# Chunk 1's second layer as seven half-size products, with batch 2's scaling of v spread over the first layer

## Chip, cores and metric

The kernel runs on one core of one Trainium2 chip. The metric is the device time of one launch in microseconds (us). Before the change it is 316.57 us, the median of 3 runs (316.44 to 317.22).

The core has five engines, each working through its own list of instructions in order: PE (TensorE: matmuls and transposes), DVE (VectorE), ACT (ScalarE), POOL (GpSimd) and SP (here only a queue that issues DMA transfers). They wait for each other by semaphores. PE writes its results into PSUM, which has eight banks; a bank can be written again only when its readers are done.

## What is computed

Attention with a decay, over 8 batches of 8 heads, 576 positions, 64 dimensions, and behind it a two-layer network with an exact GELU over all 4608 tokens:

```python
scores = scale * np.matmul(q, k.transpose(0, 1, 3, 2))
cum = np.cumsum(np.maximum(s, 0.0), axis=-1)
bias = -(cum[:, :, :, None] - cum[:, :, None, :])
scores = np.where(causal, -1000000000.0, scores + np.minimum(bias, 0.0))
attn = softmax(scores)
attn_out = np.matmul(attn, v)

x = attn_out.transpose(0, 2, 1, 3).reshape(4608, 512)
h = x @ w_in
g = 0.5 * h * (1.0 + erf(h / sqrt(2.0)))
out = g @ w_out
```

`w_in` is 512 x 2048, `w_out` 2048 x 512.

## The kernel before

**Chunks and batches.** The network runs over nine chunks of 512 tokens (`c` = 0 to 8), the attention over eight batches of 576 tokens. The loop over `c` (L748) computes chunk `c`'s two layers, and in between the attention of batch `nb = c + 1`, whose result (`xT`, a ring of 1536 token columns) the next chunks read. The order of all instructions is written out by hand; nothing is scheduled by a planner, so each engine's list is the program's order.

**First layer.** `l1_item(c, f2)` (L535) does eight matmuls of 128 x 128 by 512 columns into one of three pairs of banks X, Y, Z, and ACT applies GELU into `gT` (L551; the last item in two halves, L554). There are eight items, `f2` = 0 to 7. `order[c]` says which pair each third item takes; the same pairs hold scores and attention results in the second layer.

**Second layer, plain.** `l2_item(c, sub, f0, f1)` (L556) adds up 16 matmuls of 512 columns for each of four blocks of 128 tokens, 64 matmuls in all, into one of the single banks `M[0]`, `M[1]`; DVE or ACT copies the bank to `o_sb` and SP stores it. Chunks 0 and 1 use it.

**Second layer by seven products.** Chunks 2 to 8 split the 512 x 2048 by 2048 x 512 product into halves each way and use seven half-size products in place of eight, a Strassen-Winograd scheme. `prod(c, i, ...)` (L610) is one product: 16 matmuls of 256 columns, 112 in all. `sums_a` (L599) makes the sums of halves of `gT` on DVE (tiles `Ss`), four formulas over two halves of the inner dimension; `sums_b` (L591) made those of `w_out` (tiles `Ts`) during chunk 0. The first halves need the GELUs of items 0 to 3, the second halves those of items 4 to 7. The products share two banks: `al` (`M[0]`) is copied to `kept` three times along the way, and three additions on DVE put the output together. The `kept` tiles share buffers with the loads of q and k that batches 0 to 2 use.

**Attention of batch `nb` inside the second layer.** `sc_mm` (L421): scores of two heads into a pair of banks, exponential on ACT (L435); `mask` (L439) on DVE; `av_pe`, `av_out`, `av_tails` (L483 to L525): the product with v, logarithm and exponential on ACT, multiplication into `xT` on DVE (L498). v is first multiplied by weights of the decay: `scale_v` (L242) on DVE, reading `raw_v`, writing `vv`. `squares_v` (L233) adds up the squares of v on ACT and `absmax` (L227) the largest entries of q and k on DVE, for a certificate at the end.

**How q and k come in.** Batches 0 to 2 are transposed by PE (`tr_two`, `tr_one`, L401 to L417), batch 2 in the first layer of chunk 1: after each of the items 2 to 5, 36 transposes into the two banks `M` and two DVE copies (L399) out of them into `qkT`. Batches 3 to 7 go another way: POOL loads raw q and k (L197), casts them (`cast_qk`, L201), and at the start of the chunk before their use SP issues five DMA transposes into `qkT[nb % 2]` (`transpose_tiles`, L212). A small POOL operation behind the transposes (`behind_g`, L146, L763) holds back POOL's loads of the batch after, and a small SP transfer behind those (`behind`, L142, L792) holds back SP's loads of v (`load_v`, L220).

**Chunk 1 before.** It has a branch of its own (L892 to L919): plain second layer; all five tiles of batch 2's v are scaled after item 5 of the first layer (L778), then `squares_v(2)` and `load_v(3)`; the reductions `absmax(1, 2)` and `absmax(1, 3)` stand after the third block's matmuls (L914, L915), between the two halves of the attention.

Of the kernel before, what the change touches and what calls it, by code (L numbers as in the profile page):

```python
# [19 lines left out]
def kernel(  # L20
# [173 lines left out]
    def load_qk(b, n):  # L194
        raws[b, n] = t = work.tile([128, ST, H, D], fp32, tag=f"raw{n}", bufs=1, name=f"raw_{n}")
        for st, n_st, src in tiles(q if n == "q" else k, b):
            nc.gpsimd.dma_start(out=t[:n_st, st], in_=src)  # L197
# [22 lines left out]
    def load_v(b, engs):  # L220
        raws[b, "v"] = t = work.tile(
            [128, ST, H, D], fp32, tag="rawk" if b == 1 else "rawv", bufs=1, name="raw_v"
        )
        for st, n_st, src in tiles(v, b):
            engs[st % len(engs)].dma_start(out=t[:n_st, st], in_=src)
# [169 lines left out]
    def copy(eng, out, in_):  # L395
        if eng is nc.scalar:
            eng.copy(out, in_)
        else:
            eng.tensor_copy(out, in_)  # L399
# [348 lines left out]
    for c in range(NCH):  # L748
        nb = c + 1
        if c < 2:  # L750
            l1_item(c, 0, 0, KO - 2)
            l1_item(c, 1, 0, KO - 2)
            av_tails(c, M[0])
            l1_item(c, 0, KO - 2)
            l1_item(c, 1, KO - 2)
        else:
            l1_item(c, 0, 0, KO - 2)
            l1_item(c, 0, KO - 2)
            l1_item(c, 1)
        if 1 < c and nb < B:  # L760
            transpose_tiles(nb)
            if nb + 1 < B:
                behind_g(qkT[nb % 2][0:1, 1, NP - 1, S - 1 : S])  # L763
                for n in "qk":
                    load_qk(nb + 1, n)
        for p in range(NP) if c in (0, B - 1) else (0, 1) if c == 1 else (0, 1, 2) if c < B else ():
            absmax(c, p)
        if c == B:
            cert_1()
        for f2 in range(2, FT // 2):  # L770
            l1_item(c, f2)
            if c == 1 and 2 <= f2 < 6:
                tr_two(2, f2 // 2 - 1, f2 % 2, both)
            if c == 1 and f2 == 2:
                squares_v(1)
                load_qk(3, "k")
            if c == 1 and f2 == 5:
                scale_v(2, STS, nc.vector)  # L778
                squares_v(2)
                load_v(3, [nc.sync])  # L780
            if c == B and f2 in (2, 4):
                (cert_2, cert_3)[f2 // 2 - 1](M[0])
            if c > 1 and f2 == 3:
                if nb < B:
                    scale_v(nb, [(0, 4), (4, 5)], nc.vector)
                sums_a(c, (1, 2, 3), 0, HF // 2)
                if nb < B:
                    absmax(c, 3)
            if c > 1 and nb < B and f2 == 4:
                squares_v(nb)  # L790
                if nb + 1 < B:
                    behind(2, raws[nb + 1, "k"][0:1, ST - 2, 0, :])  # L792
                    load_v(nb + 1, [nc.sync])
        if c == 0:
            squares_v(0)
            sums_b((1, 2, 3, 4), 0, 4)
            exp_set()
            x, y, z = order[0]
            l2_item(c, 0, 0, 8)
            l2_item(c, 1, 0, 8)  # L800
            tr_one(1, 0, 0, nc.vector, z)
            tr_one(1, 0, 1, nc.scalar, x)
            l2_item(c, 2, 0, 8, y)
            sc_mm(1, 0, (z, x))
            l2_item(c, 3, 0, 8, y)
            sc_mm(1, 1, (z, x))
            mask(1, 0, nc.vector)
            sums_b((1, 2, 3), 4, 8)
            behind(1, w_out_r[0:1, FT - 5, 0:D])
            load_v(1, [nc.sync])  # L810
            l2_item(c, 0, 8, 12)
            l2_item(c, 1, 8, 12)
            tr_one(1, 1, 0, nc.vector, z)
            tr_one(1, 1, 1, nc.scalar, x)
            mask(1, 1, nc.vector)
            sums_b((4,), 4, 8)
            behind_v(1, 1)
            for qd in range(2):
                for n in "qk":
                    load_front(2, n, qd)  # L820
            l2_item(c, 2, 8, 12)
            l2_item(c, 3, 8, 12)
            sc_mm(1, 2, (z, x))
            l2_item(c, 0, 12, eng=nc.scalar)
            sc_mm(1, 3, (z, x))
            mask(1, 2, nc.vector)
            scale_v(1, STS, nc.vector)
            l2_item(c, 1, 12, eng=nc.scalar)
            l2_item(c, 2, 12, eng=nc.scalar)
            mask(1, 3, nc.vector)  # L830
            av_main(1, 0, M[0], z)
            l2_item(c, 3, 12)
            av_main(1, 1, M[1], x)
            order[1] = (y, z, x)
            load_v(2, [nc.sync])
            load_qk(3, "q")
        elif c > 1 and nb < B:
            exp_set()
            sums_a(c, (1, 2), HF // 2, HF)

            x, y, z = order[c]
            order[nb] = (z, x, y)
            add = nc.vector.tensor_tensor
            al_t = bank(M[0], [128, 2, 256], fp32, "o_al")
            al = [al_t[:, u] for u in range(2)]
            kept = [keep_sb(i, n) for i, n in enumerate(("q0", "k0", "q1"))]
            oa = [two_sb() for _ in range(2)]

            prod(c, 1, al, start=True)
            sc_mm(nb, 0, (z, x))  # L850
            sc_mm(nb, 2, (y,))
            copy(nc.vector, kept[0], al_t)
            be = bank(M[1], [128, 2, 256], fp32, "o_be")
            prod(c, 2, [be[:, u] for u in range(2)], start=True)
            prod(c, 6, al, 0, 6)
            mask(nb, 0, nc.vector)
            add(oa[0][:, :, N1], be, kept[0], op=ALU.add)
            sc_mm(nb, 2, (z,), 1)
            sc_mm(nb, 1, (x, y))
            mask(nb, 2, nc.vector)  # L860
            prod(c, 6, al, 6)
            copy(nc.vector, kept[1], al_t)
            mask(nb, 1, nc.vector)
            sc_mm(nb, 3, (z, x))
            sums_a(c, (3, 4), HF // 2, HF)
            sums_a(c, (4,), 0, HF // 2)
            ga_t = bank(M[1], [128, 2, 256], fp32, "o_ga")
            ga = [ga_t[:, u] for u in range(2)]
            prod(c, 5, ga, start=True)
            mask(nb, 3, nc.vector)  # L870
            if nb + 1 < B:
                behind_g(P_of[nb, 3][0:1, 1, PW - 1 : PW])
                cast_qk(nb + 1)
            den = bank(z, [128, 2, 512], fp32, "av_d")
            o = av_pe(nb, 0, den[:, 0], y)
            av_out(nb, 0, den[:, 0], o)
            prod(c, 7, al)
            copy(nc.scalar, kept[2], al_t)
            o = av_pe(nb, 1, den[:, 1], x)
            add(oa[1][:, :, N2], ga_t, kept[2], op=ALU.add)  # L880
            av_out(nb, 1, den[:, 1], o)
            prod(c, 4, al)
            av_tails(nb, y)
            copy(nc.scalar, oa[1][:, :, N1], al_t)
            store(c, 2, oa[1])
            prod(c, 3, ga)
            add(oa[0][:, :, N2], ga_t, kept[1], op=ALU.add)
            store(c, 1, oa[0])
            square(c + 1 if c > 2 else 0)
            if c == 2:  # L890
                cert_decay()
        elif c == 1:  # L892
            exp_set()

            x, y, z = order[c]
            order[nb] = (y, z, x)
            l2_item(c, 0, 0, 8)
            sc_mm(nb, 0, (z, x))
            sc_mm(nb, 2, (y,))
            l2_item(c, 0, 8)  # L900
            mask(nb, 0, nc.vector)
            l2_item(c, 1, 0, 3)
            sc_mm(nb, 2, (z,), 1)
            sc_mm(nb, 1, (x, y))
            mask(nb, 2, nc.vector)
            l2_item(c, 1, 3, eng=nc.scalar)
            mask(nb, 1, nc.vector)
            sc_mm(nb, 3, (z, x))
            mask(nb, 3, nc.vector)
            behind_g(P_of[nb, 3][0:1, 1, PW - 1 : PW])  # L910
            cast_qk(3)
            av_main(nb, 0, M[0], y)
            l2_item(c, 2, slot=M[1])
            absmax(1, 2)  # L914
            absmax(1, 3)  # L915
            av_main(nb, 1, M[0], z)
            l2_item(c, 3, 0, 8)
            av_tails(nb, x)
            l2_item(c, 3, 8)  # L919
        else:  # L920
            if c == B - 1:
                order[c + 1] = order[c]
            sums_a(c, (1, 2), HF // 2, HF)
            l2_seven(c)
# [156 lines left out]
```

## Time and profile before

| what | us |
|---|---|
| median of 3 runs | 316.57 |
| the profiled execution | 316.66 |
| its span in the profile | 314.8 |
| PE busy | 296.7 (94%) |
| ACT busy | 237.2 (75%) |
| DVE busy | 205.1 (65%) |
| POOL busy | 98.7 (31%) |

The profile shows one execution. "L545" is line 545 of the kernel before. A row of the timeline is: start, duration, engine, line, operation, output<-input, shapes, count, and in brackets the idle time of the engine just before, with what ended it. In rows of the chain of waits the two numbers are the start and the time that this piece contributes to the chain. PEld is PE's loading of weights, which overlaps its matmuls. SPq and POOLq rows are issues of DMA transfers; they last as long as the issue takes, not the transfer. Ends of matmuls are modelled: of 16 narrow matmuls in a row the last one's pipeline is included, so the time per matmul is read from the chain or from start to start.

### The profile page before, as it was taken

How to read it: one execution, taken by the hardware profiler on the slowest of the kernel's cores; microseconds unless marked ns; L12 is line 12 of the kernel's file. 1: busy time of each engine (PE TensorE's matmuls, PEld its weight loads, DVE VectorE, ACT ScalarE, POOL GpSimd, SP SyncE). 2: the span in 40 equal slices, each digit the busy share in tenths (PEclk: the TensorE clock that was granted, in tenths of full speed). 3: DMA queues.
4: the chain of work that ended last, by engine and by line, in shares of the span. 5: the costliest groups of instructions: out<-in, count | busy, mean ns of one | idle time of the engine just before them, and what ended most of it. 6: DMA issues, size and time to landing. Idle time of an engine off the chain costs nothing.

```text
span 314.8 us, 8169 instructions
## 1 busy us (share of the span) xinstructions
PE 296.7 (94%) x3402; PEld 183.6 (58%) x3402; DVE 205.1 (65%) x405; ACT 237.2 (75%) x322; POOL 98.7 (31%) x180
## 2 busy tenths in 40 slices
PE   1789999999999999999999999999999999999991
PEld 1564444544554578547854785478547864874680
DVE  3786357775489487797885687668765874432560
ACT  3777787799955996989698978898779885656410
POOL 6574008023080646137621953095300000000000
PEclk9999999999999999999999999999999999999997
DMA  7999999987816596959698969776990030021013
GB/s 122 208 173 198 207 194 161 294 197 186 180 38 147 132 204 132 224 100 219 132 251 124 198 144 263 137 163 139 248 188 2 2 135 0 2 94 40 2 37 106
DMA packets 77964, 45.05 MB, mean 143 GB/s; under 512 B 63200, under 2 KB 70368, under 8 KB 77920
## 3 DMA queue, kind: packets, MB, share of 16 engines
q1 hardware_dynamic: 67136, 24.93, 34.4%
q0 software_dynamic: 10784, 19.53, 32.1%
q8 instruction: 28, 0.46, 0.6%
q14 instruction: 16, 0.13, 0.2%
HBM read 36.85 MB, written 9.44 MB: 147 GB/s over the span
## 4 chain that ended last, share of the span: by engine, by line
PE 85%; ACT 5%; DVE 4%; DMA 2%; issue 1%; POOL 0%; ACTq 0%; POOLq 0%
PE h_ps L545 39%; PE o_al L617 16%; PE o_ga L617 8%; PE o_ps L569 5%; PE sc_ps L429 5%; PE o_be L617 4%; PE av_o L458 4%; PE av_d L458 2%; DMA fk<-in_k_dram 2%; ACT junk L237 2%; ACT P L435 2%; DVE vv L247 2%; PE av_t L458 1%; PE tr_ps L390 1%; DVE qkT L399 1%
## 5 line engine op out<-in xcount | busy, mean ns | idle before, releaser
L545 PE MATMUL h_ps<-xT,w_in_r 128*128 128x512 bf16 x576 | 127.1, 379 | 0.5 <-DVE o_sb L399 0.5
L545 PEld LDWEIGHTS <-w_in_r 128*128 128x128 bf16 x576 | 55.7, 98 | 65.5 <-issue 0.8
L551 ACT ACTIVATE gT<-h_ps 128x1024 f16<-128x1024 f32 x63 | 62.7, 1020 | 24.7 <-PE h_ps L545 24.5
L435 ACT ACTIVATE P<-sc_ps 128x1024 bf16<-128x1024 f32 x64 | 60.3, 1030 | 3.2 <-PE sc_ps L429 3.2
L617 PEld LDWEIGHTS <-S 128*128 128x128 f16 x448 | 42.1, 98 | 6.7 <-issue 0.8
L229 DVE TENSOR_REDUCE amx<-qkT 128x2 f32<-128x1152 bf16 x32 | 41.5, 1344 | 0.1
L608 DVE TENSOR_TENSOR S<-gT 128x1024 f16<-128x1024 f16 x28 | 19.3, 688 | 31.3 <-ACT gT L554 24.0
L617 PEld LDWEIGHTS <-gT 128*128 128x128 f16 x336 | 32.0, 98 | 7.1 <-issue 1.8
L443 DVE TENSOR_TENSOR P<-P,tri_bf 128x512 bf16<-128x512 bf16 x64 | 25.9, 421 | 14.0 <-ACT P L435 13.5
L569 PE MATMUL o_ps<-w_out_r,gT 128*128 128x512 f16 x128 | 30.0, 380 | 0.0
L617 PE MATMUL o_al<-T,S 128*128 128x256 f16 x224 | 27.7, 273 | 0.0
L197 POOL DMA_DIRECT2D raw_k<-in_k_dram x25 | 21.1, 850 | 13.5 <-DMA raw_v<-in_v_dram 13.5
L429 PE MATMUL sc_ps<-qkT 64*128 64x256 bf16 (+2 forms) x320 | 22.2, 264 | 3.0 <-DVE qkT L399 1.7
L498 DVE TENSOR_TENSOR xT<-av_o,ln 128x256 bf16<-128x256 f32 (+2 forms) x72 | 23.6, 387 | 2.1 <-ACT ln L474 0.9
L247 DVE TENSOR_TENSOR vv<-raw_v,wb 128x512 bf16<-128x512 f32 (+2 forms) x25 | 23.7, 1001 | 0.0
L197 POOL DMA_DIRECT2D raw_q<-in_q_dram x25 | 21.1, 858 | 0.9 <-POOL seen_v L148 0.6
L429 PEld LDWEIGHTS <-qkT 64*128 64x128 bf16 x320 | 13.8, 99 | 12.6 <-issue 7.0
L237 ACT ACTIVATE junk<-raw_v 128x2048 bf16<-128x2048 f32 (+1 forms) x16 | 20.3, 1269 | 0.3
L569 PEld LDWEIGHTS <-gT 128*128 128x128 f16 x128 | 11.5, 98 | 13.6 <-issue 0.7
L399 DVE COPY qkT<-tr_ps 128x576 bf16<-128x576 bf16 (+1 forms) x15 | 12.0, 834 | 9.4 <-PE tr_ps L390 9.4
L474 ACT ACTIVATE ln<-ln,lnb 128x256 f32<-128x256 f32 x32 | 16.3, 510 | 1.0
L458 PE MATMUL av_o<-P,vv 128*32 128x256 bf16 (+1 forms) x512 | 16.8, 273 | 0.0
(114 smaller groups left out, 335.7 us busy)
## 6 DMA issues: line engine op xcount, KB each, us to landing
raw_v<-in_v_dram SPq DMA_DIRECT2D x32, 256.0 KB, 5.0
out_dram<-o_sb SPq DMA_DIRECT2D x12, 512.0 KB, 4.0
raw_q<-in_q_dram POOLq DMA_DIRECT2D x20, 256.0 KB, 4.7
raw_k<-in_k_dram POOLq DMA_DIRECT2D x20, 256.0 KB, 6.2
out_dram<-o_sb SPq DMA_DIRECT2D x11, 256.0 KB, 3.7
w_out_r<-in_moe_w_out_dram POOLq DMA_DIRECT2D x4, 512.0 KB, 13.2
fq<-in_q_dram POOLq DMA_DIRECT2D x6, 288.0 KB, 7.1
fk<-in_k_dram POOLq DMA_DIRECT2D x6, 288.0 KB, 8.2
```

The source lines that it names most:

```text
L197: nc.gpsimd.dma_start(out=t[:n_st, st], in_=src)
L229: nc.vector.tensor_reduce(amx[:, b * NP + p], qkT[b % 2][:, :, p, :S], axis=AX, op=ALU.max, apply_absolute_value=True)
L237: nc.scalar.activation(n[:n_st, : (st1 - st0) * H * D], t[:n_st, st0:st1].rearrange("p s h d -> p (s h d)"), func=AF.Square, accum_out=amv ...
L247: eng.tensor_tensor(vb[:n_st, st0:st1, h0:h1, :], t[:n_st, st0:st1, h0:h1, :], wb[:n_st, st0:st1, b * H + h0 : b * H + h1] .unsqueeze(3).t ...
L429: nc.tensor.matmul(s_ps[:, e, off : off + n], lhsT=qkT[b % 2][e * 64 : e * 64 + 64, 1, p, jt * 128 : jt * 128 + 128], rhs=qkT[b % 2][e * 6 ...
L435: nc.scalar.activation(P[:, :, UO[u] : UO[u] + UW[u]], s_ps[:, :, : UW[u]], func=AF.Exp, scale=scale)
L443: eng.tensor_tensor(d, d, tri_bf.unsqueeze(1).unsqueeze(1).to_broadcast([128, 2, 2, 128]), op=MULT)
L458: nc.tensor.matmul(o[g * 32 : g * 32 + 32, lo : lo + n], lhsT=(wb[:, jt, b * H + 2 * g + qd : b * H + 2 * g + qd + 1].to_broadcast([128, 3 ...
L545: nc.tensor.matmul(h_ps[:, i, :], lhsT=w_in_r[:, ko, ft * 128 : (ft + 1) * 128], rhs=xT[:, ko, c * NB % XW : c * NB % XW + NB], start=(ko ...
L551: nc.scalar.activation(gT_of[c][:, f2 * 2 : f2 * 2 + 2, :], h_ps, func=AF.Gelu)
L569: nc.tensor.matmul(o_ps, lhsT=gT[:, ft, sub * 128 : (sub + 1) * 128], rhs=w_out_r[:, ft], start=(ft == 0), stop=(ft == FT - 1),)
L617: nc.tensor.matmul(o[u], lhsT=lhs[:, f, u * 128 : u * 128 + 128], rhs=rhs[:, f], start=start and f == 0 and (by_sub or u == 0), stop=f == ...
```

## The change

Chunk 1's own branch is deleted; chunk 1 now runs the branch of chunks 2 to 6 with seven products. Around it four things are particular to chunk 1:

- Batch 2's q and k are still transposed by PE in the first layer.
- Its v is scaled tile by tile: tile 0 after item 3's copies, tile 1 after item 4's, tiles 2 and 3 after item 5's copies and the first-half sums, tile 4 in the second layer, behind the copy of the first product (`kept[0]`).
- `load_v(3)` is issued behind that last tile.
- `absmax(1, 2)` and `absmax(1, 3)` come at the end of the layer, in the place where later chunks run `square` on ACT.

The banks' order for chunk 2 changes from `(y, z, x)` to the `(z, x, y)` that the other chunks use.

```diff
             if c == 1 and f2 == 2:
                 squares_v(1)
                 load_qk(3, "k")
+            if c == 1 and 3 <= f2 < 5:
+                scale_v(2, STS[f2 - 3 : f2 - 2], nc.vector)
             if c == 1 and f2 == 5:
-                scale_v(2, STS, nc.vector)
+                sums_a(c, (1, 2, 3), 0, HF // 2)
+                scale_v(2, STS[2:4], nc.vector)
                 squares_v(2)
-                load_v(3, [nc.sync])
...
-        elif c > 1 and nb < B:
+        elif nb < B:
             exp_set()
             sums_a(c, (1, 2), HF // 2, HF)
...
             copy(nc.vector, kept[0], al_t)
+            if c == 1:
+                scale_v(2, STS[4:5], nc.vector)
+                load_v(3, [nc.sync])
...
             store(c, 1, oa[0])
-            square(c + 1 if c > 2 else 0)
+            if c == 1:
+                absmax(1, 2)
+                absmax(1, 3)
+            else:
+                square(c + 1 if c > 2 else 0)
             if c == 2:
                 cert_decay()
-        elif c == 1:
-            exp_set()
-            x, y, z = order[c]
-            order[nb] = (y, z, x)
-            l2_item(c, 0, 0, 8)
-            sc_mm(nb, 0, (z, x))
-            sc_mm(nb, 2, (y,))
-            l2_item(c, 0, 8)
...
-            l2_item(c, 2, slot=M[1])
-            absmax(1, 2)
-            absmax(1, 3)
-            av_main(nb, 1, M[0], z)
-            l2_item(c, 3, 0, 8)
-            av_tails(nb, x)
-            l2_item(c, 3, 8)
```

More of the change, by code (lines that the diff above doesn't have):

```diff
@@ L888 @@
             store(c, 1, oa[0])
-            square(c + 1 if c > 2 else 0)
+            if c == 1:
[3 more added lines that the diff above has]
+                square(c + 1 if c > 2 else 0)
             if c == 2:
                 cert_decay()
-        elif c == 1:
-            exp_set()
-            x, y, z = order[c]
-            order[nb] = (y, z, x)
-            l2_item(c, 0, 0, 8)
-            sc_mm(nb, 0, (z, x))
-            sc_mm(nb, 2, (y,))
-            l2_item(c, 0, 8)
[L901 to L912, printed above, removed]
-            l2_item(c, 2, slot=M[1])
-            absmax(1, 2)
-            absmax(1, 3)
-            av_main(nb, 1, M[0], z)
-            l2_item(c, 3, 0, 8)
-            av_tails(nb, x)
-            l2_item(c, 3, 8)
         else:
```

## The prediction

> **What bounds the kernel now.** I read the page first, then stage windows, then the chain of waits, then the timeline around chunk 1.
>
> ```profile
> span 314.8 us, 8169 instructions
> PE 296.7 (94%) x3402; PEld 183.6 (58%) x3402; DVE 205.1 (65%) x405; ACT 237.2 (75%) x322; POOL 98.7 (31%) x180
> ...
> PE 85%; ACT 5%; DVE 4%; DMA 2%; issue 1%; POOL 0%; ACTq 0%; POOLq 0%
> ...
> L617 PEld LDWEIGHTS <-S 128*128 128x128 f16 x448 | 42.1, 98 | 6.7 <-issue 0.8
> ```
>
> PE is busy 94% of the span and makes up 85% of the chain that ended last, so time taken from PE counts unless PE then waits. The next view cuts the trace at first matmuls: 75.03 and 108.76 begin the second layers of chunks 1 and 2, 94.95 the first layer of chunk 2.
>
> ```profile
> core 0: us, PE busy (x) PEld busy (x) DVE busy (x) ACT busy (x) POOL busy (x), PEclk, DMA share, GB/s
> 75.03:94.95 19.92, 19.61 (x249) 10.01 (x248) 12.12 (x31) 15.88 (x24) 6.54 (x17) 1.00 0.48 112
> 94.95:108.76 13.81, 13.81 (x65) 6.26 (x64) 10.51 (x10) 9.46 (x12) 3.78 (x5) 1.00 0.62 132
> 108.76:126.96 18.20, 18.20 (x297) 14.68 (x296) 12.53 (x30) 15.65 (x25) 11.30 (x24) 1.00 0.83 174
> ```
>
> The old second layer of chunk 1 takes 19.92. Chunk 2 runs the seven products with the scores and attention of one batch in 18.20, at the same granted clock of 1.00. So the trace holds a measured model of the stage that chunk 1 gets. What must be added is how chunk 1 differs: its engines arrive in another state.
>
> ```profile
> 72.19 2.00 ACT junk L237 x2
> ...
> 75.84 0.96 ACT gT L554 x2
> ...
> 78.12 2.86 ACT P L435 x3
> ...
> 81.02 0.40 PE sc_ps L429 x6
> ...
> 95.11 13.81 PE h_ps L545 x64
> 108.93 1.75 PE o_al L617 x16
> ```
>
> In chunk 1 the chain leaves PE between 72 and 81: the squares of v (L237), the last GELUs, and the first three exponentials run one after the other on ACT until PE's scores get their bank at 81.02. ACT, not PE, sets that point.
>
> **The change part by part.** *Products.* Removed: 64 products of 512 columns; added: 112 of 256. From the chain, 13.81 / 64 = 0.216 for the wide and 1.75 / 16 = 0.109 for the narrow: 13.81 - 12.25 = 1.56 saved. The stages differ by 19.92 - 18.20 = 1.72, 0.16 more. I take the stage, because it contains the changes of bank and operand too.
>
> The Trainium skill ("TensorE: Matmul & The Clock Gate", "Back-to-back issue gap") speaks against this: in a stream of loads and matmuls it gives 131 ns for 512 columns and 81 ns for 128. The trace disagrees, at 216 and 109 ns. A straight line between the page's figures, my estimate, puts 256 columns at 98 ns; 64 x 131 = 8.4 us would then become 112 x 98 = 11.0 us, a loss of 2.6 us where the trace gives a gain of 1.56.
>
> *ACT arrives late.* The next rows give the loads of v (issue and landing), then both stages.
>
> ```profile
> raw_v<-in_v_dram SPq DMA_DIRECT2D x32, 256.0 KB, 5.0
> ...
> 58.97 1.42 SPq L225 DMA_DIRECT2D raw_v<-in_v_dram  x2
> ...
> 69.45 1.42 DVE L399 COPY qkT<-tr_ps 128x576 bf16<-128x576 bf16 x2 [0.82 <-PE tr_ps L390]
> ...
> 73.03 3.08 DVE L247 TENSOR_TENSOR vv<-raw_v,wb 128x512 bf16<-128x512 f32 x5
> ...
> 75.03 1.89 PE L569 MATMUL o_ps<-w_out_r,gT 128*128 128x512 f16 x8
> 75.75 1.06 ACT L554 ACTIVATE gT<-h_ps 128x512 f16<-128x512 f32 x2
> ...
> 108.76 1.91 PE L617 MATMUL o_al<-w_out_r,gT 128*128 128x256 f16 x16
> 109.17 1.06 ACT L554 ACTIVATE gT<-h_ps 128x512 f16<-128x512 f32 x2
> ...
> 110.26 0.69 DVE L608 TENSOR_TENSOR S<-gT 128x1024 f16<-128x1024 f16 x1 [3.86 <-ACT gT L554]
> ...
> 111.60 0.68 DVE L399 COPY kept<-o_al 128x512 f32<-128x512 f32 x1
> ...
> 113.13 0.82 PE L617 MATMUL o_al<-T,S 128*128 128x256 f16 x6
> 113.88 0.97 PE L429 MATMUL sc_ps<-qkT 64*128 64x256 bf16 x16
> ```
>
> The last GELU ends 109.17 + 1.06 - 108.76 = 1.47 after PE enters the layer in chunk 2, and 75.75 + 1.06 - 75.03 = 1.78 in chunk 1: 0.31 later. In the model PE reaches the scores 113.88 - 108.76 = 5.12 into the stage, here 80.15; after ten of the sixteen (0.97 / 16 each, 0.61) it would want the bank of the third exponential at 80.76, but ACT releases it at 81.02, as now. PE waits some 0.26 to 0.31, and at the next scores the fifth exponential is as late, so nothing is won back. The bounds are 0 (if the model had slack there) and 0.31; I take 0.31. The layer then takes 18.51, and chunk 2 starts at 93.54 instead of 94.95: **1.41 saved**. ACT's later releases are as in the model, relative to PE.
>
> *Pieces of v between the copies.* A piece costs 3.08 / 5 = 0.62. The copies of one round end 1.42 after they start, and the row shows DVE idle 0.82 before the round at 69.45: a piece fits with 0.2 over. Without that cover two pieces would delay the transposes behind them by at most 1.24. The first two tiles of v are wanted at 68.6 and 70.9, up to 4.4 earlier than now; they were issued by 60.39 and such a load lands after 5.0 by the median. Pieces and first-half sums then run from 69.45 + 2.24 + 1.42 = 73.11: 3 x 0.69 + 2 x 0.62 = 3.31, to 76.42, and the second-half sums cannot start before the last GELU at 76.81 anyway. Cost 0.
>
> *The copy of the first product* (kept[0]). In chunk 2 it ends 111.60 + 0.68 = 112.28, 2.05 after the last GELU; here 76.81 + 2.05 = 78.86. The product that overwrites the bank starts 4.37 into the model (113.13), here 79.40: 0.54 of slack, against 0.85. The last piece of v follows at 78.86 to 79.48; the first mask behind it could start at 78.12 + 2.86 / 3 = 79.07 and so loses 0.41, but the second waits for the next exponential until 80.03 in any case. Cost 0; with the slack gone, PE would wait as long as the copy is late. Two copies, three additions and five sums replace three copies; DVE goes from 12.12 to about 13.5 in 18.5 (chunk 2's 12.53, the piece, and a little for columns of xT split at the ring's end). DVE is no bound.
>
> *The loads of v for batch 3*, five issues on SP, move from the end of the scaling (73.03 + 3.08 = 76.1) to 79.5. Behind them SP has only stores, four of half the size before and two now, the first after the seventh product. Their reader, chunk 2's scaling, comes at about 100.9 (below). Cost 0, with over 15 of cover. POOL issues the same list in the same order.
>
> *The two amax reductions* leave the middle of the layer for its end, and this adds a wait: batch 3's transposes overwrite what they read.
>
> ```profile
> 90.35 2.60 DVE L229 TENSOR_REDUCE amx<-qkT 128x2 f32<-128x1152 bf16 x2
> ...
> 95.76 3.86 DVE L229 TENSOR_REDUCE amx<-qkT 128x2 f32<-128x1152 bf16 x3
> 96.32 6.82 SPq L215 DMA_TRANSPOSE qkT<-qk_bf  x5
> ...
> 104.84 0.34 POOL L148 CAST seen_v<-qkT 1x1 f32<-1x1 bf16 x1 [10.76 <-DMA qkT<-qk_bf]
> ...
> 110.60 0.55 PEld L429 LDWEIGHTS <-qkT 64*128 64x128 bf16 x14 [0.21 <-issue]
> ...
> 120.26 5.27 SPq L225 DMA_DIRECT2D raw_v<-in_v_dram  x5
> ...
> 126.56 1.71 SPq L632 DMA_DIRECT2D out_dram<-o_sb  x2
> 128.37 8.14 SPq L215 DMA_TRANSPOSE qkT<-qk_bf  x5
> ...
> 138.82 0.35 POOL L148 CAST seen_v<-qkT 1x1 f32<-1x1 bf16 x1 [11.57 <-DMA qkT<-qk_bf]
> ...
> 160.42 9.39 SPq L215 DMA_TRANSPOSE qkT<-qk_bf  x5
> 171.56 0.18 POOL L148 CAST seen_v<-qkT 1x1 f32<-1x1 bf16 x1 [12.30 <-DMA qkT<-qk_bf]
> 193.20 8.14 SPq L215 DMA_TRANSPOSE qkT<-qk_bf  x5
> 204.56 0.18 POOL L148 CAST seen_v<-qkT 1x1 f32<-1x1 bf16 x1 [13.29 <-DMA qkT<-qk_bf]
> ```
>
> DVE is done with the last product 95.76 - 94.95 = 0.81 into chunk 2 (an addition stands where the copy stood): 94.4; the reductions end 2.60 later (97.0), so the transposes start at 97.1: 0.8 later on the clock, 2.1 later against PE. How long they take to land isn't shown for a start there. From start to POOL's note it was 8.5 in chunk 2 and 10.5, 11.1, 11.4 in chunks 3 to 5, where two stores go just ahead of them (126.56 to 128.27). Here these stores go some 2.7 ahead, so I take the near row, 8.5, and keep 10.5 and more for the rivals: landed at 105.6. The scores need them at 110.60 - 1.41 = 109.2.
>
> Behind them hangs a loop: POOL's loads of batch 4 wait for the landing, SP's loads of v wait for those, the stores and the next transposes wait on SP behind these. A landing s later than 104.84 ends SP's loads of v at 125.53 + s and starts the next transposes 128.37 - 126.56 = 1.81 after that, at 127.34 + s. Scores recur every 13.81 + 18.20 = 32.01. With the landings of chunks 3 to 5, and starts 32.05 and 32.78 apart as now, the waits of the scores sum to s - 3.41 by chunk 3, s - 2.68 by chunk 4 and s - 1.69 by chunk 5 (203.53 + s landed, 206.63 - 1.41 needed), none where this is negative. With s = 0.8 they are 0, with 0.9 over. Cost 0; without that cover, a microsecond for each microsecond.
>
> On DVE the 2.60 push what follows in chunk 2: its reductions end at 97.0 + 3.86 = 100.9, and all behind them is as late, up to the second-half sums; there DVE was idle 3.86 (the row at 110.26). Cost 0; without that idle time 2.60.
>
> The sum: -1.72 + 0.31 = **-1.41**. The profiled execution took 316.66 (span 314.8 and 1.86 around it), so 315.25; it lay 0.09 over the median, so I predict 315.2.
>
> **The rivals.** (a) ACT's lateness costs nothing: -1.72, 314.9. For it: the wait is only inferred from offsets; against it: the chain itself runs through ACT here.
> (b) DVE decides. Its queue is fullest between 73.1 and 79.5; each delay over 0.54 before the copy of the first product stalls PE. One piece and one addition more (1.3) would cost 0.8: 316.0. Against it: the second-half sums wait for ACT, with 0.39 idle by my walk.
> (c) The loop takes most of it back: chunk 2's transposes land as chunk 3's did, 10.5 after their start, at 107.6. Then s is 2.7 and the scores of chunk 5 have waited 1.0: 316.3. For it: the same two stores go out in this stage. Against it: they are 2.7 away.
> (d) Slower: the same loop, thrown further. With a landing 12.4 after the start, one more than chunk 5's, s is 4.7; the waits come to 3.0, net 1.6 slower: 318.2. It decides from s = 3.1, a landing at 107.9, on; below that the change keeps something. For it: landing slips from 9.9 to 13.6 into the chunk between chunks 2 and 5, so the loop is slower than PE. Against it: no row has 12.4.
> (e) The products don't get cheaper: weight loads come to light. 48 more at 98 ns are 4.7, net 3.3 slower, 319.9. Against it: 16 narrow products with 16 loads take 1.75. By the Trainium skill's section named above the end would be near 319.4.
>
> **How the numbers follow.** Forecast 0.62, (a) 0.07, (b) 0.12, (c) 0.12, (d) 0.06, (e) 0.01. What a measurement can tell from no change is 0.3%, 0.95 us: faster means below 315.6. The forecast, (a) and half of (b) lie there: 0.75. Half of (b) and (c): 0.18. (d) and (e): 0.07. The range takes in (a) with 0.3 of spread below, 314.6, and (b) and (c) with 0.1 above, 316.4; (d) and (e) are left out.
>
> **What would show it.** Right: in the changed profile the stretch from the first L617 to the next L545 in chunk 1 lasts 18.5, all 112 products at 0.109; ACT's third exponential still ends near 81.0 with PE waiting there; DVE's copy of kept[0] ends near 78.9; batch 3's transposes start near 97.1; no score waits for qkT in chunks 2 to 6; later chunks keep 32.0; the second batch of DMA transposes starts near 128.1. Wrong: PE idle before the third product with DVE as releaser (b), or PE idle before L429 with a transpose as releaser (c, d), or first-layer rounds of chunk 1 over 2.24 (1.42 + 0.82) apart because a copy came behind a piece of v.

## The result and the profile after

| what | us |
|---|---|
| median after, 6 runs (314.50 to 314.81) | 314.61 |
| median before beside them, 6 runs (316.44 to 317.22) | 316.73 |
| ratio, with its 95% interval | 0.9932 [0.9919, 0.9945] |
| span of the profiled execution, before and after | 314.8, 312.9 |

The change makes the kernel 2.12 us faster. The prediction had 1.41, and 315.2 for the time. On the basis of the 316.57 that it started from, the ratio gives 314.4, which lies 0.2 under the lower end of the range. Direction, stage and mechanism came out as forecast; the question of the experiments is where the rest of the gain comes from.

The page of the changed kernel gives its span and busy times; the last two rows are pieces of its chain of waits.

```profile
span 312.9 us, 8245 instructions
...
PE 293.8 (94%) x3428; PEld 187.6 (60%) x3450; DVE 211.6 (68%) x415; ACT 237.6 (76%) x323; POOL 98.6 (32%) x180
...
81.05 0.40 PE sc_ps L429 x6
...
107.52 1.75 PE o_al L617 x16
```

PE still makes up most of the chain that ended last (81%, before 85%), and sixteen narrow matmuls take the same 1.75 as before. The windows of the changed kernel (the columns as in the prediction's windows) show the second layers of chunks 1 and 2.

```profile
75.06:93.55 18.49, 18.23 (x298) 14.66 (x297) 14.60 (x38) 15.92 (x25) 6.45 (x17) 1.00 0.42 79
107.36:125.56 18.20, 18.20 (x298) 14.68 (x297) 12.62 (x30) 15.65 (x25) 13.42 (x26) 1.00 0.83 174
```

Chunk 1's stage went from 19.92 to 18.49 (forecast 18.51), and chunk 2's stayed at 18.20, all at the granted clock of 1.00. Where the 0.29 between the two stages lies is seen in the timeline of the changed kernel, with the steps that the prediction walked through:

```profile
68.58 0.68 DVE L247 TENSOR_TENSOR vv<-raw_v,wb 128x512 bf16<-128x512 f32 x1
69.48 1.42 DVE L399 COPY qkT<-tr_ps 128x576 bf16<-128x576 bf16 x2 [0.22 <-PE tr_ps L390]
...
74.99 1.29 DVE L247 TENSOR_TENSOR vv<-raw_v,wb 128x512 bf16<-128x512 f32 x2
75.06 1.91 PE L617 MATMUL o_al<-w_out_r,gT 128*128 128x256 f16 x16
75.78 1.06 ACT L554 ACTIVATE gT<-h_ps 128x512 f16<-128x512 f32 x2
76.87 0.69 DVE L608 TENSOR_TENSOR S<-gT 128x1024 f16<-128x1024 f16 x1 [0.59 <-ACT gT L554]
...
78.20 0.68 DVE L399 COPY kept<-o_al 128x512 f32<-128x512 f32 x1
79.43 0.82 PE L617 MATMUL o_al<-T,S 128*128 128x256 f16 x6
...
81.05 0.40 PE L429 MATMUL sc_ps<-qkT 64*128 64x256 bf16 x6 [0.26 <-ACT P L435]
...
93.55 13.98 PE L545 MATMUL h_ps<-xT,w_in_r 128*128 128x512 bf16 x62
...
108.86 0.69 DVE L608 TENSOR_TENSOR S<-gT 128x1024 f16<-128x1024 f16 x1 [2.13 <-ACT gT L554]
```

Read from the top: the piece of v leaves 0.22 of the idle 0.82 before the copies. The second-half sums wait for the last GELU (0.59 idle), so DVE is early, not late. The copy of `kept[0]` ends at 78.88, the third product starts at 79.43, with no wait in brackets. PE waits once, 0.26 before the scores at 81.05, for ACT's exponential. In chunk 2 the second-half sums still have 2.13 of idle time (3.86 before), so the later start of DVE's work there is covered.

The loop of batch 3, in the same kernel:

```profile
97.05 6.84 SPq L215 DMA_TRANSPOSE qkT<-qk_bf  x5
105.55 0.18 POOL L148 CAST seen_v<-qkT 1x1 f32<-1x1 bf16 x1 [11.91 <-DMA qkT<-qk_bf]
109.20 0.83 PE L429 MATMUL sc_ps<-qkT 64*128 64x256 bf16 x14
...
120.88 4.34 SPq L225 DMA_DIRECT2D raw_v<-in_v_dram  x5
125.33 2.13 SPq L632 DMA_DIRECT2D out_dram<-o_sb  x2
127.56 6.70 SPq L215 DMA_TRANSPOSE qkT<-qk_bf  x4
```

The transposes land 3.65 ahead of the scores, and PE does not wait there.

What the stage does not explain is found by cutting both profiled executions at the same marks: the starts of the first weight load of the first layers of chunks 1 and 3, the end of DVE's last copy, and the end of the span.

| stretch | before | after | difference |
|---|---|---|---|
| start to chunk 1's first layer | 58.03 | 58.07 | +0.04 |
| chunks 1 and 2 | 68.83 | 67.38 | -1.45 |
| chunk 3 to DVE's last copy | 181.61 | 181.60 | -0.01 |
| the copy to the end of the span | 6.32 | 5.83 | -0.49 |

Chunks 1 and 2 hold the 1.45 (to 0.01 by rounding); 0.49 lies behind the last copy. There one row stands out, the last store of SP, in the timeline of before and then of after:

```profile
308.50 1.04 SPq L632 DMA_DIRECT2D out_dram<-o_sb  x1
```

```profile
307.08 0.34 SPq L632 DMA_DIRECT2D out_dram<-o_sb  x1
```

The issue of the same store is 0.70 shorter. The change edits nothing at this place, so the first runs ask whether it reaches there.

### The profile page after: what moved, and what is told of

Its sections match the earlier page's. It is cut to its first block, busy times and chain, and to the rows that moved or that the text cites. A ratio compares the mean times of both kernels' runs of the same rounds, so it can differ in the third digit from the quotient of the medians.

```text
span 312.9 us, 8245 instructions
## 1 busy us (share of the span) xinstructions
PE 293.8 (94%) x3428; PEld 187.6 (60%) x3450; DVE 211.6 (68%) x415; ACT 237.6 (76%) x323; POOL 98.6 (32%) x180
## 4 chain that ended last, share of the span: by engine, by line
PE 81%; DMA 8%; ACT 5%; DVE 2%; issue 2%; POOL 1%; SPq 0%; ACTq 0%; POOLq 0%
PE h_ps L545 36%; PE o_al L617 18%; PE o_ga L617 9%; PE sc_ps L429 5%; DMA w_in_r<-in_moe_w_in_dram 4%; PE o_be L617 4%; PE av_o L458 3%; DMA raw_v<-in_v_dram 2%; PE av_d L458 2%; PE o_ps L569 2%; ACT junk L237 2%; ACT P L435 2%; DMA fq<-in_q_dram 2%; PE av_t L458 1%; DVE vv L247 1%
## 5 line engine op out<-in xcount | busy, mean ns | idle before, releaser
L545 PE MATMUL h_ps<-xT,w_in_r 128*128 128x512 bf16 x554 | 125.8, 379 | 1.9 <-DVE o_sb L399 0.5
L617 PEld LDWEIGHTS <-S 128*128 128x128 f16 x512 | 48.1, 98 | 7.7 <-issue 0.9
L608 DVE TENSOR_TENSOR S<-gT 128x1024 f16<-128x1024 f16 x32 | 22.0, 687 | 29.0 <-ACT gT L554 22.8
L617 PEld LDWEIGHTS <-gT 128*128 128x128 f16 x384 | 36.5, 98 | 8.2 <-issue 2.2
L617 PE MATMUL o_al<-T,S 128*128 128x256 f16 x256 | 31.7, 273 | 0.0
L197 POOL DMA_DIRECT2D raw_k<-in_k_dram x25 | 21.1, 850 | 13.5 <-DMA raw_v<-in_v_dram 13.5
L397 ACT COPY kept<-o_al 128x512 f32<-128x512 f32 (+1 forms) x15 | 7.5, 501 | 13.8 <-PE o_al L617 10.4
L148 POOL CAST seen_v<-qkT 1x1 f32<-1x1 bf16 x4 | 1.0, 240 | 50.2 <-DMA qkT<-qk_bf 50.2
L207 POOL CAST qk_bf<-raw_k 128x512 bf16<-128x512 f32 (+1 forms) x40 | 16.4, 499 | 0.0
```

The costliest lines, as they stand in the source:

```text
L545: nc.tensor.matmul(h_ps[:, i, :], lhsT=w_in_r[:, ko, ft * 128 : (ft + 1) * 128], rhs=xT[:, ko, c * NB % XW : c * NB % XW + NB], start=(ko ...
L608: nc.vector.tensor_tensor(o, u, w, op=op)
L617: nc.tensor.matmul(o[u], lhsT=lhs[:, f, u * 128 : u * 128 + 128], rhs=rhs[:, f], start=start and f == 0 and (by_sub or u == 0), stop=f == ...
```

## The experiments

### Is the end of the kernel faster by the change, or by chance?

The first four runs are both kernels again and two variants of the changed one: one restores the number of stores ahead of the last one, one adds instructions on PE.

`before_again`: the kernel before, unchanged.

> The kernel before, unchanged, profiled once more. Question: of the 2.1 us that the change gained, the stage of chunk 1 explains 1.41; 0.70 lies after the last product, where the issue of the last store on SP took 1.04 us in the one profile of before and 0.34 in the one of after. Theory S (it belongs to the program, by where its instruction fetches or its queue stand at the end): the last issue takes about 1.0 us again and the span is 314.8 within 0.3. Theory R (chance of one profile): the last issue takes about 0.35 us, and the span is near 314.1. Times: 316.4 to 317.2 either way, ratio 1.000.

Measured: 316.95 (12 runs) against 317.14 for the runs of the same kernel beside it, ratio 0.9991 [0.9971, 1.0012]. Its last store took 0.72, neither the 1.0 of theory S nor the 0.35 of theory R, and its end 6.00.

`after_again`: the changed kernel, unchanged.

> The changed kernel, unchanged, profiled once more. Theory S: the issue of the last store takes about 0.35 us again, ratio to before 0.993. Theory R: it may take 0.35 or 1.0. Both: the second layer of chunk 1 from its first narrow product to the next first-layer matmul 18.5 us, products of chunk 8 ending 1.4 earlier than in before.

Measured: 315.20 (6 runs), ratio 0.9943 [0.9925, 0.9960]. The last store took 0.94, nearly as slow as in the first trace of before, and the end 6.13. Chunk 1 took 35.36 from first layer to first layer, as in the first trace of the change.

`after_four_stores`: chunk 1's two stores of 512 KB are issued as four of 256 KB, as before.

```diff
-            store(c, 2, oa[1])
+            for u in range(2 if c == 1 else 1):
+                store(c, 2, oa[1], subs=slice(u, u + 1) if c == 1 else slice(0, 2))
...
-            store(c, 1, oa[0])
+            for u in range(2 if c == 1 else 1):
+                store(c, 1, oa[0], subs=slice(u, u + 1) if c == 1 else slice(0, 2))
```

> The changed kernel with chunk 1's two stores of 512 KB issued as four of 256 KB, so that SP's list has as many DMA issues as before the change; bytes and sums are the same. Theory Q (the place in SP's queue decides the last issue): the last issue takes 1.0 us again and the time is 0.7 above after, 315.3. Theory P (PE's instruction stream decides it) and R: the last issue stays at 0.35 and the time at 314.6.

Measured: 315.52 (6 runs), ratio 0.9955 [0.9938, 0.9973]; the last store took 1.02.

`after_pe_160_more`: 80 transposes of a constant, each with its weight load, ahead of the first transposes of q and k.

```diff
+    spare = bank(M[1], [128, 16, 64], bf16, "spare")
+    for i in range(80):
+        nc.tensor.transpose(spare[0:64, i % 16, :], ident_bf[0:64, 0:64], ident_bf[0:64, 0:64])
     tr_one(0, 0, 0, nc.scalar, X)
```

> The changed kernel with 80 small transposes (160 instructions on PE) of a constant tile at the very start, into a bank that is overwritten later, so that PE's list is the old one plus 256 instructions: PE's fetches of 16 KB, about 256 instructions apart in the trace, then stand at the end as they stood in before. PE is idle for most of the place, the transposes take about 1.5 us there and the chain may move by 0 to 0.5. Theory P: the last issue takes 1.0 us again, time 315.3 to 315.8. Theories Q and R: it stays at 0.35, time 314.6 to 315.1.

Measured: 318.13 (8 runs), ratio 1.0036 [1.0022, 1.0050]; the last store took 1.12. This is well over the 314.6 to 315.8 that the theories allowed. The added transposes kept PE busy for 4.37 where 1.5 was expected, and the first transposes of q started at 9.10 instead of 6.02. The first weight load of the first layer moved to 23.65, 1.3 to 2.5 later than in the other traces: the added work lies on the path of the front, and this is most of its price. The execution also lost 0.63 in chunk 5.

What follows: the unchanged kernel after had 0.34 in one execution and 0.94 in the next, so the 1.04 against 0.34 is no property of the change. Neither the number of stores nor PE's count of instructions is needed for a slow one.

The traces do show what a slow one goes with. In all fourteen a packet of 16 KB, on the queue that the page lists as "q8 instruction", is under way when this store is issued. In the three with 0.34 it starts 0.12 to 0.15 before the store. In the other eleven it starts 0.65 to 0.83 before, and the store's issue ends 0.37 to 0.44 after the packet does. That the issue waits for this packet fits, but no run tests it.

### Times and traces again

`after_third`: the changed kernel once more, with its own runs of before beside it.

> The changed kernel once more, beside the next three kernels. Every theory: chunk 1's second layer 18.5 us, later chunks 32.01 apart. If the remainder over 1.41 is scatter of front and end, the ratio to before lies between 0.993 and 0.9955 and the issue of the last store anywhere from 0.35 to 1.1.

Measured: 315.23 (8 runs), ratio 0.9950 [0.9932, 0.9969], last store 0.67.

`before_third`, `before_fourth` and `after_fourth`: one execution of each, for their traces.

> The kernel before, unchanged, for its trace: the front (first matmul of the first layer), the end (last copy of DVE to the end of the span), the chunk periods and idle stretches of PE inside the products with the values of v. Theory (the 0.2 to 0.7 us that after gained beyond 1.44 are scatter of the execution): the periods of chunks 1 and 2 stay 36.7 and 32.1 to within 0.3, while front and end move by some tenths without regard to the kernel: the front in 21 to 22.5, the end in 5.6 to 6.5 as in the traces so far. Rival (the kernel before loses time in a place of its own): the same place, with the same price of 0.3 or more, in each of its traces and in none of after's.

> As the run before it: a further trace of the kernel before. Theory: front and end move by some tenths against the other traces of the same kernel, the periods of chunks 1 and 2 stay. Rival: one place that loses 0.3 or more in all traces of before.

> The changed kernel, unchanged, for its trace beside the two of before on the same chip. Theory: chunk 1 takes 35.37 and chunk 2 32.01, 1.44 less than before in all, and front and end lie in the same bands as those of before (21 to 22.5 and 5.6 to 6.5). Rival (the change also shortens the front or the end): this trace's front or end lies below both of before's by 0.3 or more.

Measured: 315.83, 315.89 and 315.46, one run each. With the earlier ones this makes four traces of each kernel. "Chunk 1 starts" is its first weight load of the first layer; the periods run to the next chunk's; "later" is the sum of the waits beyond 32.01 in chunks 3 to 6; "end" runs from DVE's last copy to the end of the span.

| trace | span | chunk 1 starts | chunk 1 | chunk 2 | later | last store | end |
|---|---|---|---|---|---|---|---|
| before | 314.8 | 58.03 | 36.70 | 32.12 | 0 | 1.04 | 6.32 |
| before_again | 315.1 | 58.14 | 36.70 | 32.12 | 0.51 | 0.72 | 6.00 |
| before_third | 314.0 | 58.21 | 36.70 | 32.12 | 0 | 0.34 | 5.31 |
| before_fourth | 314.1 | 57.83 | 36.70 | 32.12 | 0 | 0.88 | 5.85 |
| after | 312.9 | 58.07 | 35.37 | 32.01 | 0 | 0.34 | 5.83 |
| after_again | 313.4 | 58.31 | 35.36 | 32.01 | 0 | 0.94 | 6.13 |
| after_third | 312.8 | 58.17 | 35.37 | 32.01 | 0 | 0.67 | 5.61 |
| after_fourth | 313.7 | 58.58 | 35.36 | 32.01 | 0 | 0.90 | 6.11 |

Chunks 1 and 2 give 68.81 or 68.82 in all four traces of before, 67.37 or 67.38 in all four of after: some 1.44 saved, the same each time. (That chunk 2's period is 0.11 shorter comes from the mark: in the first two traces the first weight load of its first layer starts 0.21 before its matmul in before, and 0.11 in after.) The front and the end scatter by more than the kernels differ there. The mean end is 5.87 before and 5.92 after. One of before's lies at 5.31, below the 5.6 to 6.5 that was expected of it, so the band was still too narrow. The spans differ by 1.3 in the mean (314.5 and 313.2). No place costs before 0.3 or more in all its traces, so the rival falls; the 0.51 of `before_again` are two stretches of its own in the attention. Both of them, then a similar one in `after_pe_160_more`, in their timelines:

```profile
154.10 1.17 PE L458 MATMUL av_o<-P,vv 128*32 128x256 bf16 x32
...
221.20 0.70 PE L458 MATMUL av_t<-P,vv 128*32 128x64 bf16 x32
```

```profile
221.41 0.28 PE L458 MATMUL av_t<-P,vv 128*32 128x64 bf16 x13
222.14 0.33 PE L458 MATMUL av_t<-P,vv 128*32 128x64 bf16 x19 [0.45 <-issue]
```

The 32 matmuls take 1.17 instead of 0.94 and 0.70 instead of 0.43, or stop for 0.45 between the 13th and the 14th. "Issue" means that the profile names nothing that held PE. The traces have a sign here too: a 16 KB packet of the queue "q8 instruction" ends a little earlier. In the four traces of before and in `after_pe_160_more`, the one in chunk 5 ends 28.3, 28.5 and 28.7 after the chunk's first weight load where nothing is lost, 29.0 where 0.28 is lost and 29.5 where 0.63 is lost. In chunk 3 it ends at 24.5 to 25.3 in four of them without loss, and at 26.7 in `before_again`, which loses 0.23. PE waiting for a late packet would explain this; no run tests it.

One rival stays open with it. These losses were seen only in a trace of before and in `after_pe_160_more`, whose expectation counts PE's list as that of before plus 256 instructions, one such packet; in none of the four traces of after. All three comparisons of the unchanged kernels lie above 1.44 (2.12, 1.94 and 1.72 between the medians). So a few tenths that the change gains by shifting where in PE's list these packets fall are not ruled out.

### Is ACT's lateness the term that keeps chunk 1 above the model?

`squares_after_item_4`: the squares of batch 2's v are issued on ACT one item earlier, so that the last GELUs do not come behind them.

```diff
             if c == 1 and 3 <= f2 < 5:
                 scale_v(2, STS[f2 - 3 : f2 - 2], nc.vector)
+                if f2 == 4:
+                    squares_v(2)
...
-                squares_v(2)
```

> The changed kernel with batch 2's squares of v one first-layer item earlier on ACT. Theory A (ACT's lateness of 0.31 costs PE a wait before the scores): ACT does the squares at 70.4 instead of 72.2, the last GELU ends about 1.05 after PE enters the layer instead of 1.78, PE's wait near 81 of 0.26 goes, chunk 1's second layer takes 18.1 to 18.2 instead of 18.5, and the time falls by 0.3 to 0.4 against after. Rival (the wait only moves to the next bank or to DVE's copy): the layer stays at 18.4 to 18.5.

Its timeline around the entry of the layer and the start of chunk 2:

```profile
75.86 1.91 PE L617 MATMUL o_al<-w_out_r,gT 128*128 128x256 f16 x16
...
76.06 1.08 ACT L554 ACTIVATE gT<-h_ps 128x512 f16<-128x512 f32 x2 [0.28 <-PE h_ps L545]
...
80.98 0.83 PE L429 MATMUL sc_ps<-qkT 64*128 64x256 bf16 x16
...
94.06 2.11 PE L545 MATMUL h_ps<-xT,w_in_r 128*128 128x512 bf16 x8
```

The last GELU now ends 77.14 - 75.86 = 1.28 after PE enters the layer; in the changed kernel it was 75.78 + 1.06 - 75.06 = 1.78. ACT itself is idle 0.28 before it, waiting for PE. The sixteen scores run in one row without a wait, and the stage takes 94.06 - 75.86 = 18.20, the model's time to the hundredth. So the 0.29 was the price of ACT's lateness, as the prediction had it. The period of chunk 1 is 35.09 instead of 35.36. In the times this isn't visible: 315.35 (10 runs, 314.49 to 317.11), ratio 0.9958 [0.9935, 0.9980], against 315.23 for the changed kernel beside it. The expected fall of 0.3 to 0.4 in the whole time is not seen; it is smaller than the spread of these runs.

### What do the pieces of v cover?

`pieces_all_after_item_5`: all five tiles stay together after item 5, where before had them, behind the first-half sums.

```diff
-            if c == 1 and 3 <= f2 < 5:
-                scale_v(2, STS[f2 - 3 : f2 - 2], nc.vector)
             if c == 1 and f2 == 5:
                 sums_a(c, (1, 2, 3), 0, HF // 2)
-                scale_v(2, STS[2:4], nc.vector)
+                scale_v(2, STS, nc.vector)
                 squares_v(2)
...
             if c == 1:
-                scale_v(2, STS[4:5], nc.vector)
                 load_v(3, [nc.sync])
```

> The changed kernel with all five tiles of batch 2's v scaled in a row after item 5 and the first sums. Theory D (DVE has about 0.5 of slack before the copy of the first product, and PE's wait for ACT behind it absorbs a part): DVE's scaling ends at 78.2, the second-half sums at 79.5, the copy of kept[0] at 80.2; the third product starts 0.8 late, PE's wait for the third exponential goes, and chunk 1's second layer takes 18.9 to 19.1 instead of 18.5. Rival (the waits add up): 19.3. Rival (DVE has more slack than that): 18.5.

Its timeline:

```profile
75.18 3.08 DVE L247 TENSOR_TENSOR vv<-raw_v,wb 128x512 bf16<-128x512 f32 x5
75.26 1.91 PE L617 MATMUL o_al<-w_out_r,gT 128*128 128x256 f16 x16
78.19 0.68 DVE L608 TENSOR_TENSOR S<-gT 128x1024 f16<-128x1024 f16 x1
...
79.51 0.68 DVE L399 COPY kept<-o_al 128x512 f32<-128x512 f32 x1
...
80.25 0.81 PE L617 MATMUL o_al<-T,S 128*128 128x256 f16 x6 [0.47 <-DVE kept L399]
...
81.44 2.85 ACT L435 ACTIVATE P<-sc_ps 128x1024 bf16<-128x1024 f32 x3 [0.24 <-PE sc_ps L429]
...
94.08 2.11 PE L545 MATMUL h_ps<-xT,w_in_r 128*128 128x512 bf16 x8
```

Now DVE decides. The sums come at 78.19 instead of 76.87 (0.20 of it because this execution enters the stage later), the copy of `kept[0]` ends at 80.19, and PE waits 0.47 before the third product, with DVE as the releaser. In exchange the wait for ACT is gone: PE comes to the scores so late that ACT waits for it. The stage takes 94.08 - 75.26 = 18.82, 0.33 more than with the pieces spread (period 35.72, +0.36). That is somewhat under the expected 18.9 to 19.1. The third product starts 80.25 - 75.26 = 4.99 into the stage, 0.62 later than the model's 4.37, and the stage is 0.62 over the model's 18.20: the wait for DVE is paid in place of the wait for ACT (0.29), not besides it. The single run took 315.61.

### What does the loop of the transposes cost when it is late?

`two_more_reductions`: the two amax reductions at the end of chunk 1 are done twice.

```diff
             if c == 1:
                 absmax(1, 2)
                 absmax(1, 3)
+                absmax(1, 2)
+                absmax(1, 3)
```

> The changed kernel with the two reductions at the end of chunk 1's second layer done twice (the same values again), 2.6 more on DVE ahead of batch 3's transposes. Theory L (the loop of transposes and loads has 1.7 of slack up to chunk 5): transposes start at 99.7 and land near 108.2, 3.3 later than in before; the scores of chunks 3 to 5 wait for transposes, 1.6 in all, 316.2 to 316.8. Rival (more slack, the loop catches up by itself): no score waits, time as after, 314.6 to 315.2. Third way (DVE): the second-half sums of chunk 2 start 0.45 late, which 0.85 of slack before the third product covers.

Its timeline, from the transposes in chunk 2 to the scores of chunk 6:

```profile
100.20 6.82 SPq L215 DMA_TRANSPOSE qkT<-qk_bf  x5
109.90 0.62 POOL L148 CAST seen_v<-qkT 1x1 f32<-1x1 bf16 x1 [15.66 <-DMA qkT<-qk_bf]
109.84 0.83 PE L429 MATMUL sc_ps<-qkT 64*128 64x256 bf16 x14
...
125.18 5.28 SPq L225 DMA_DIRECT2D raw_v<-in_v_dram  x5
130.58 1.07 SPq L632 DMA_DIRECT2D out_dram<-o_sb  x2
131.75 8.39 SPq L215 DMA_TRANSPOSE qkT<-qk_bf  x5
...
141.83 0.40 POOL L148 CAST seen_v<-qkT 1x1 f32<-1x1 bf16 x1 [13.97 <-DMA qkT<-qk_bf]
141.85 0.83 PE L429 MATMUL sc_ps<-qkT 64*128 64x256 bf16 x14
...
206.56 0.51 PE L429 MATMUL sc_ps<-qkT 64*128 64x192 bf16 x8 [0.20 <-DMA qkT<-qk_bf]
...
239.21 0.51 PE L429 MATMUL sc_ps<-qkT 64*128 64x192 bf16 x8 [0.28 <-DMA qkT<-qk_bf]
```

The transposes start 3.15 later than in the changed kernel, and land 4.35 later, since they take 9.70 to POOL's note instead of 8.50. The note at 109.90 even comes 0.06 after the scores have begun, without a wait. Nothing is lost in chunks 2, 3 and 4. In chunks 5 and 6 PE waits for a transpose, and the periods are 32.39 and 32.64: 0.38 and 0.63, together 1.01. The time agrees: 316.40 (10 runs), ratio 0.9987 [0.9968, 1.0007], 0.0037 over `after_third` beside it, 1.2 us. It lies in the expected 316.2 to 316.8, but not for the expected reason: the waits were to stand in chunks 3 to 5, and the landing near 108.2.

This execution as a whole runs 0.63 behind that of the changed kernel (chunk 2 starts at 94.18 and 93.55). By the prediction's formula, with s = 109.90 - 104.84 - 0.63 = 4.43, chunk 3 would have waited 1.02 and chunk 5 have lost 2.74 in all, where 0.38 was measured. So rivals (c) and (d) rest on a mechanism that exists, at far too high a price. The rows show three reasons. The formula puts 1.81, measured from the first store to the transposes, behind the loads of v, as if it were fixed; here SP's loads end at 130.46 and the transposes start 1.29 later. In chunk 3 they land 10.08 after their start (141.83 - 131.75), not 10.5. And the formula stops PE at POOL's note, which reads the last of the five tiles, while the scores that began when the note came did not wait.

### Shape or number of columns?

`before_narrow_products`: the kernel before, with chunk 1's 64 wide matmuls as 128 of half the width.

```diff
-            nc.tensor.matmul(
-                o_ps, lhsT=gT[:, ft, sub * 128 : (sub + 1) * 128],
-                rhs=w_out_r[:, ft], start=(ft == 0), stop=(ft == FT - 1),
-            )
+            for n0, n1 in ((0, 512),) if c == 0 else ((0, 256), (256, 512)):
+                nc.tensor.matmul(
+                    o_ps[:, n0:n1], lhsT=gT[:, ft, sub * 128 : (sub + 1) * 128],
+                    rhs=w_out_r[:, ft, n0:n1], start=(ft == 0 and n0 == 0), stop=(ft == FT - 1),
+                    skip_group_check=True,
+                )
```

> The kernel before, with one edit: each of the 64 matmuls of 512 columns in chunk 1's second layer is issued as two of 256 columns on the two halves of the same bank (128 matmuls and 128 weight loads, the same sums). It parts the two things that the change does to these products: fewer columns of work (7/8) and a narrower matmul. Theory (a matmul costs its columns, and the weight loads stay hidden, 0.109 us for 256 columns as in chunk 2's rows): 128 x 0.109 = 13.95 against 64 x 0.216 = 13.8, so the stage from the first L569 to the next L545 takes 19.9 to 20.2 (19.92 before), and the gain of the change came from 7/8 of the products alone. Rival (weight loads come to light as there are more of them, 0.098 us each): 64 more, up to 6.3 us longer, about 26. By the Trainium skill, "TensorE: Matmul & The Clock Gate", "Back-to-back issue gap", 131 ns for 512 and 81 for 128 columns, an estimate on a straight line between them of 98 ns for 256: 128 x 98 against 64 x 131 would be 4.2 us longer; the trace has had 216 and 109 so far.

Its timeline:

```profile
75.47 1.91 PE L570 MATMUL o_ps<-w_out_r,gT 128*128 128x256 f16 x16
...
81.45 0.40 PE L429 MATMUL sc_ps<-qkT 64*128 64x256 bf16 x6 [0.26 <-ACT P L435]
...
109.31 1.91 PE L619 MATMUL o_al<-w_out_r,gT 128*128 128x256 f16 x16
```

From the first product of chunk 1 to the first of chunk 2 it takes 109.31 - 75.47 = 33.84, against 108.76 - 75.03 = 33.73 with wide matmuls: 0.11 for twice as many matmuls and weight loads. (The row of chunk 2's first layer starts at 95.71 and gives a stage of 20.24, 0.04 beyond the expected band. The weight loads start at 95.39, 0.32 earlier, where the other traces have 0.11 to 0.21, so its first matmul is missing from the trace; the longer stretch avoids this.) The wait of 0.26 for ACT is there in the plain layer as well. So the products cost their columns to within 0.11, and the gain of the change comes from the eighth of the columns that seven products for eight save: sixteen narrow matmuls of 128, 1.75. Of these, 0.11 goes to the width and 1.43 is measured as the stage's gain; the last 0.2 no run parts. Rival (e) falls. The estimate from the Trainium skill's figures ("TensorE: Matmul & The Clock Gate", "Back-to-back issue gap") was 4.2 for this edit; the run shows 0.11. The single run took 317.13.

## Why the prediction was right, and where it was wrong

**Products: right.** The stage fell by 1.43 (1.41 forecast), narrow matmuls cost 0.109, and `before_narrow_products` shows that their number and shape add 0.11 at most.

**ACT's lateness: right.** 0.31 was taken, 0.29 is the difference of the stages, PE's wait stands at 81.05 (forecast 81.02), and with the squares moved ahead it is gone, and the stage is the model's 18.20. Rival (a) falls.

**Pieces of v: right that they cost nothing where they stand.** The copies kept 0.22 of idle time (0.2 forecast). `pieces_all_after_item_5` shows the cover at work from the other side: with it gone DVE stalls PE, rival (b)'s mechanism, for 0.33 of stage where (b) had 0.8 by another delay. The copy of the first product comes 1.11 later there (4.93 into the stage instead of 3.82) and the third product 0.62, so the slack is 0.49 where the prediction had 0.54.

**The copy of the first product: right.** It ended at 78.88 (78.86), and the third product started at 79.43 (79.40). The figure for DVE's load in the stage was off, 14.60 where the text had 13.5: 1.22 of the two pieces of v (74.99 to 76.28) lies inside the stage, as in the prediction's own walk, and its sum left them out. DVE wasn't the bound, so the time did not feel it.

**The loop: right in its result** (start 97.05 against 97.1, landing 105.55 against 105.6, no wait). The next transposes came at 127.56, not near 128.1. With s = 0.71 the formula ends the loads of v at 126.24 and starts the transposes 1.81 later. The rows show the loads ending at 125.22, since their five issues took 4.34 instead of 5.27, and the transposes 2.34 later. Two errors partly cancel here, and the 1.81 is no fixed price: it was 1.29 in `two_more_reductions`.

**What failed is the sum's base and its spread**: "-1.41. The profiled execution took 316.66 (span 314.8 and 1.86 around it), so 315.25", and in the range "0.3 of spread below". It took all time outside chunk 1 for fixed and gave 0.3 for what that scatters. The four traces of each kernel show that it isn't: the end ranges over 5.31 to 6.32, chunk 1's start over 57.83 to 58.58. The profiled execution of before, which the sum was made against, had the longest end of all eight. The forecast saving of 1.41 compares with 1.44 in the traces, so the term for the stage was right. The later ratios, 0.9943 [0.9925, 0.9960] and 0.9950 [0.9932, 0.9969], have 1 - 1.44 / 316.7 = 0.9955 within their intervals, and on the basis of 316.57 they give 314.8 and 315.0, inside the range; the first, 0.9932 [0.9919, 0.9945], has not. About 0.7 of its 2.12 is thus outside chunks 1 and 2. That executions scatter by such an amount is shown, in the end, the front and the stretches in the attention. Why the six first runs of after all lay between 314.50 and 314.81 is not: only one of them has a trace, whose end accounts for 0.49 against its partner. Whether a part of the 0.7 belongs to the change stays open.

## What to carry to other kernels

A later stage of the same kernel that already runs the new code is a better price list than counts of instructions, if one adds how the engines arrive: here the model's 18.20 plus ACT's lateness gave 18.51 for 18.49. The profile of one execution gives differences inside a stage to some hundredths, but its front and end are one draw; a range for the whole time needs their spread, from several executions. The loop of queues here forgave most of a lateness of 4 us: check which transfer the reader really waits for before charging a microsecond for each microsecond.

## What the runs showed of the hardware that was not expected

- The issue of one and the same last store on SP took between 0.34 and 1.04 in eight executions of two kernels, and 0.34 to 1.22 in the six variants. The slow issues go with a 16 KB packet of the queue "q8 instruction" that starts 0.65 to 0.83 before the store; the issue then ends 0.37 to 0.44 after the packet. The span's end does not follow the issue closely (5.83 with 0.34, 5.61 with 0.67).
- PE lost 0.23 to 0.63 in a stretch of small attention matmuls in two executions of fourteen, without a wait that the profile could name; each time the packet of that queue before it ended later than in the traces without loss (29.0 and 29.5 against 28.3 to 28.7 into chunk 5).
- Five DMA transposes of the same size took 8.50 from issue to POOL's note when started 3.5 into the first layer of chunk 2 (97.05 - 93.55), and 9.70 when started 6.0 into it (100.20 - 94.18).
